# Attention with two feed-forward layers on one core: part of the weight split moved to GpSimd, four raw buffers, held-back stores and a re-planned order

## The chip, the cores and the metric

The kernel runs on one core of one Trainium2 chip. The metric is the device time of one execution in microseconds (us). Engines are named as in the profile: PE is TensorE, DVE is VectorE, ACT is ScalarE, POOL is GpSimd, SP is SyncE, which here only issues DMAs.

## The reference

```python
def reference(**kwargs):
    attn_out = _attn_ref(q, k, v)                 # q, k, v: (4, 8, 576, 64)
    x = attn_out.transpose(0, 2, 1, 3).reshape(B * S, H * D)     # (2304, 512)
    x = _moe_ref(x, moe_w_in, moe_w_out)          # relu(x @ w_in) ** 2 @ w_out
    return _moe2_ref(x, moe2_w_in, moe2_w_out)    # softplus(x @ w_in) @ w_out

# _attn_ref: softmax attention on q, k, v averaged over groups of 4 tokens (144 of them),
# its result repeated 4 times, plus softmax attention over the band |i - j| < 4.
# w_in: (512, 2048), w_out: (2048, 512), all float32.
```

All of it is float32. On PE each product of float32 numbers is made from a high part and a low part in a reduced format (`F32R`): high times high, high times low and low times high, so every weight and every activation is first split in two.

## The kernel before, in words

**Tiles and steps.** The 2304 tokens are 36 groups of 64, cut into five blocks of 8, 6, 6, 8 and 8 groups (`BLOCKS`). A step is one block, one layer and one slice `f` of 128 of the 2048 hidden units: `hidden` multiplies the tokens by that slice of `w_in` (12 matmuls, line 1501), `activate` and `split` make the two parts of the result on ACT and DVE, and `outputs` multiplies by the slice of `w_out` (12 matmuls, line 1585). 106 such steps come first, then two phases that need fewer products (line 1443). Steps 0 to 9 are the first layer on block 0 with the slices 0 to 7, steps 10 to 25 the first layer on block 1.

**Attention.** For blocks 0 and 1 the banded part runs as matmuls (`local`), and so does the pooled part of every batch (`pooled` and `pooled_twos`; their scores are at lines 808 and 894); for blocks 2 to 4 the banded part is done on DVE (`direct`). Block 1 needs the pooled part of batch 1, whose keys, queries and values are added up over 4 tokens by DMAs that accumulate (`token_sums_of`, issued on POOL, line 758).

**Weights.** A slice of a layer's weights is 2 halves (`w_in` and `w_out`), and there are 64 halves. The input holds them as 64-bit numbers. `load_weights` fetches a half of 512 KB into one of `RAWS` buffers (SP, line 500), `weight_job` then does three operations on the raw words, each on ACT or DVE (lines 517 to 533; either engine for the first `ANY_JOBS` halves, ACT alone after that), two on DVE (537 and 540), a copy that makes the high part (either engine) and a subtraction that makes the low part:

```python
copy(w[:, 0], f.tile)
t = yield "dve", t_dve(512)
rest(w[:, 1], f.tile, w[:, 0])
```

The finished half is written to DRAM (SP, line 554), because SBUF has 8 slots for weights, and `weight_again` fetches it from there when it is wanted again (POOL, line 570). `f` has 3 buffers, freed by the subtraction.

**Order.** Nothing is scheduled at run time: each engine's queue is in order, and `Order.run` writes the queues beforehand from a model. Every piece of work is a generator that yields the engine it wants, the time that it is reckoned to take, and what it needs; of what could start first, the planner takes the earliest, then the most urgent. The constants at the top (`LOCAL`, `POOLED`, `U_...`, `NUDGE`, `BIAS`, `AT_ONCE`, `PREP_DVE`, the times behind `yield "pe"`) set urgencies and reckoned times and so the order, not what is computed. `AHEAD` says how many steps ahead of its use a half may be begun. `keep_busy` (line 1206) puts a matmul of the identity, which nobody reads, into PE's queue wherever the model sees PE idle, until step 12; each shows as two instructions. What is in the queue is executed even if PE is late by then.

## Time and profile before

| what | value |
|---|---|
| median of 3 runs | 864.97 us (863.11 to 865.01) |
| the profiled execution | 864.84 us |
| its span, from first to last instruction | 862.9 us |
| matmuls | 4724 |

The profiled execution is 1.9 us longer than its span, and within 0.2 us of the median. In the rows below, times are from the start of the span. A busy PE is not PE at its peak: matmuls are pipelined and their ends are modelled, so the start of one matmul to the start of the next says how long it holds PE.

### The profile page before, as it was taken

Reading aid. Unit: us, or ns where it says so; the run is one execution under the profiler, and the core shown is the slowest. Engines: PE = TensorE matmul, PEld = TensorE weight load, DVE = VectorE, ACT = ScalarE, POOL = GpSimd, SP = SyncE. Lnnn points to the kernel's source line nnn. Section 1 sums busy time; section 2 is a strip of 40 time slices with the busy share of each in tenths; the row PEclk is TensorE's granted clock in tenths of the full one; section 3 lists DMA queues with packets and bytes.
Section 4 is the critical chain, followed back from the end, with each engine's and each line's share of the span. In section 5 each row is a group of like instructions: output and inputs, shape, how many; then the busy total and the mean of one; then the engine's idle time right before and its main releaser. Section 6 shows DMA issues by size and latency. Waiting matters only on the chain.

```text
span 862.9 us, 12987 instructions
## 1 busy us (share of the span) xinstructions
PE 854.3 (99%) x4724; PEld 735.0 (85%) x4724; DVE 691.4 (80%) x1272; ACT 505.3 (59%) x1058; POOL 90.6 (10%) x163
## 2 busy tenths in 40 slices
PE   8999999999999999999999999999999999999998
PEld 5788799988888888899999998888888888888886
DVE  6988989989999899999979999954657497675543
ACT  4967878766997797542336444534454076676500
POOL 0100000010002000122221212012000201100010
PEclk9999999999999999999999999999999999999999
DMA  9996699897769863699995986335210835510161
GB/s 283 243 342 212 228 333 340 299 260 283 262 229 290 288 233 151 192 344 307 295 304 178 309 283 208 118 123 170 74 50 4 283 104 196 157 39 0 52 193 49
DMA packets 49575, 179.20 MB, mean 208 GB/s; under 512 B 5790, under 2 KB 6302, under 8 KB 49512
## 3 DMA queue, kind: packets, MB, share of 16 engines
q1 hardware_dynamic: 27336, 97.92, 32.3%
q0 software_dynamic: 22032, 80.32, 30.9%
q8 instruction: 37, 0.61, 0.3%
q14 instruction: 26, 0.21, 0.1%
q10 hardware_dynamic: 144, 0.13, 0.0%
HBM read 140.08 MB, written 38.27 MB: 207 GB/s over the span
## 4 chain that ended last, share of the span: by engine, by line
PE 98%; DVE 1%; DMA 1%; ACT 0%; issue 0%; SPq 0%; DVEq 0%
PE y L1585 45%; PE ph L1501 28%; PE p L1443 15%; PE idle L1206 1%; PE lsc L996 1%; PE ppo L955 1%; PE lav L1052 1%; PE y L1616 1%; PE ppp L938 1%; PE lpp L1042 1%; PE psc L808 1%; PE dpp L1174 1%; PE psc L894 0%; DMA w_first<-pqk 0%; PE ppo L860 0%; PE ppp L840 0%
## 5 line engine op out<-in xcount | busy, mean ns | idle before, releaser
L1501 PE MATMUL ph<-xh,w 128*128 128x384 f32 (+2 forms) x848 | 248.0, 355 | 0.0
L1585 PE MATMUL y<-gh,w 128*128 128x512 f32 (+2 forms) x640 | 191.0, 365 | 0.2 <-DVE lt L1060 0.2
L1585 PE MATMUL y<-w,gh 128*128 128x512 f32 x576 | 179.4, 392 | 0.0
L1501 PEld LDWEIGHTS ph<-xh,w 128*128 128x128 f32 x848 | 155.7, 188 | 13.7 <-issue 0.2
L1501 PE MATMUL ph<-xl,w 128*128 128x384 f32 (+2 forms) x424 | 149.5, 353 | 0.0
L1585 PEld LDWEIGHTS y<-gh,w 128*128 128x128 f32 x640 | 118.0, 188 | 14.6 <-DVE lt L1060 0.3
L1585 PEld LDWEIGHTS y<-w,gh 128*128 128x128 f32 x576 | 106.8, 188 | 21.9 <-issue 1.0
L570 POOL DMA_DIRECT2D w<-wdram x138 | 73.8, 536 | 483.1 <-PE y L1585 251.1
L1585 PE MATMUL y<-gl,w 128*128 128x512 f32 (+2 forms) x320 | 115.9, 362 | 0.0
L1585 PE MATMUL y<-w,gl 128*128 128x512 f32 x288 | 112.6, 391 | 0.0
L449 DVE TENSOR_TENSOR gl<-g,gh 128x512 fp32r<-128x512 f32 (+2 forms) x162 | 101.9, 629 | 5.2 <-ACT gh L436 2.2
L1501 PEld LDWEIGHTS ph<-xl,w 128*128 128x128 f32 x424 | 79.7, 188 | 6.8
L438 DVE CAST gh<-g 128x512 fp32r<-128x512 f32 (+2 forms) x81 | 32.8, 405 | 50.3 <-PE y L1585 44.4
L1517 ACT ACTIVATE g<-ph 128x384 f32<-128x384 f32 (+2 forms) x58 | 30.3, 522 | 69.8 <-PE ph L1501 69.6
L1585 PEld LDWEIGHTS y<-gl,w 128*128 128x128 f32 x320 | 60.2, 188 | 6.6
L436 ACT ACTIVATE sum<-p 128x512 f32<-128x512 f32 x42 | 24.8, 590 | 69.0 <-PE p L1443 68.9
L436 ACT ACTIVATE gh<-g 128x384 fp32r<-128x384 f32 (+2 forms) x81 | 46.1, 569 | 30.6 <-PE y L1585 18.2
L1585 PEld LDWEIGHTS y<-w,gl 128*128 128x128 f32 x288 | 54.0, 188 | 11.5
L1527 ACT ACTIVATE g<-ph 128x384 f32<-128x384 f32 (+1 forms) x48 | 25.1, 523 | 44.2 <-PE ph L1501 43.9
L1470 DVE TENSOR_TENSOR sum<-p,sum 128x512 f32<-128x512 f32 x42 | 28.9, 687 | 25.4 <-ACT sum L436 17.4
L1160 DVE TENSOR_TENSOR prod<-dv,dsc 128x896 f32<-128x896 f32 x44 | 47.9, 1089 | 0.6
L1167 DVE TENSOR_REDUCE do<-prod 128x128 f32<-128x896 f32 x44 | 47.7, 1084 | 0.8
(183 smaller groups left out, 1428.9 us busy)
## 6 DMA issues: line engine op xcount, KB each, us to landing
w<-wdram POOLq DMA_DIRECT2D x138, 512.0 KB, 4.7
raw<-wts SPq DMA_DIRECT2D x64, 512.0 KB, 5.8
wdram<-w SPq DMA_DIRECT2D x64, 512.0 KB, 5.3
dqk<-dqk SPq DMA_DIRECT2D x11, 896.0 KB, 6.0
dv<-dv SPq DMA_DIRECT2D x11, 640.0 KB, 6.5
qks<-pqs POOLq DMA_DIRECT2D x9, 576.0 KB, 9.3
out<-o SPq DMA_DIRECT2D x17, 256.0 KB, 2.3
vs<-pvs POOLq DMA_DIRECT2D x9, 288.0 KB, 9.4
```

What stands on the lines that cost most here:

```text
L436: act.activation(out=out, in_=in_, func=AF.Copy)
L438: dve.tensor_copy(out=out, in_=in_)
L449: dve.tensor_tensor(out=out, in0=whole, in1=high.bitcast(F32), op=ALU.subtract)
L570: nc.gpsimd.dma_start(out=weights[slot][:, half], in_=wdram[c, half])
L1160: dve.tensor_tensor(out=p4, in0=windows(v4[:, h], 2, t0, p4.shape[1]), in1=s4[:, t0:t0 + some, h].unsqueeze(2).to_broadcast(list(p4.shape) ...
L1167: dve.tensor_reduce(out=o4[:, t0:t0 + some, h], in_=p4, axis=AX.X, op=ALU.add)
L1443: pe.matmul(bank.tile, w, y, start=(k == 0 and p in (1, 2, 5)), stop=(k == len(prs) - 1), skip_group_check=True)
L1470: dve.tensor_tensor(out=b.tile, in0=bank.tile, in1=b.tile, op=ALU.add)
L1501: pe.matmul(ph.tile[:, :n], w, y, start=(k == 0), stop=(k == len(prs) - 1))
L1517: act.activation(out=o, in_=h, func=AF.Relu)
L1527: act.activation(out=o, in_=h, func=AF.Abs)
L1585: pe.matmul(o, wt, y, start=(begin and k == 0), stop=(end and k == 2))
```

## The change

The order constants are set anew (many `NUDGE` entries, `LOCAL`, `BIAS`, `AT_ONCE`, `U_MLP`, `AHEAD`, and the reckoned times of several groups of matmuls). Beside the order, this is changed:

- `RAWS` goes from 3 to 4.
- The stores of halves that belong to steps 0 to 3 (two slices, four halves) are issued once step 4 has begun by the plan; `slot_free` now also tells the planner that a slot can be filled again only when its old content is stored.
- The three raw operations can go to either engine for 40 halves, not 28, and DVE is reckoned at 0.35 for each, not 0.6.
- The first layer's activation can go to either engine for steps below 32 (`BOTH_TO`), not none.
- For the last 36 of the 64 halves (`REST_FROM` is 28) the subtraction that makes the low part is done by POOL.
- The sums of batch 1 begin with the fourth raw load, not the third; those of batches 2 and 3 wait for step 30, not 24. A pair of banded tasks shares its loads whichever of the two comes first.

```diff
--- before.py
+++ after.py
@@ -118,29 +118,32 @@
 
 
 POOLED = [(-20, -17), (-0.6, -0.4), (31, 42), (46, 56)]
-LOCAL = [(-17, -13), (0.5, 6), (14, 46), (46, 64), (58, 74)]
+LOCAL = [(-17, -13), (-2, 4), (14, 46), (46, 64), (58, 74)]
 BY_TWOS = [1, 2, 3]
 
-U_MLP, U_WEIGHTS, U_ATT, U_DIRECT = -2, 0.5, 1, 20
-AHEAD = 10
+U_MLP, U_WEIGHTS, U_ATT, U_DIRECT = -3, 0.5, 1, 20
+AHEAD = 14
 EARLY = 2
 SLOTS = 8
 LENT = 5
 
-RAWS, FLOATS = 3, 3
+RAWS, FLOATS = 4, 3
+STORE_FROM = 4
+REST_FROM, POOL_REST = 28, 1.3
+SUMS_FROM = 3
 LAG = 1
-ANY_JOBS = 28
-PREP_DVE = 0.6
+ANY_JOBS = 40
+PREP_DVE = 0.35
 OUTS = 3
 BUFS = dict(q=2, v=3, s=3, e=4, t=5, pt=2, n=6, do=5)
 BUFS["in"] = 2
 
 LAT = 0.15
-BIAS = 0.1
-NUDGE = {(12, 0): -1, 7: -5, 2: -2, 11: -5, 3: -5, (3, 1): 4, ('l', 2, None): 40, (7, 0): -4, 14: 5, (11, 1): -2, 9: -2, 20: 5, ('at', 2, 2): -0.5}
+BIAS = 0.25
+NUDGE = {7: -5, 3: -5, (3, 1): 4, ('l', 2, None): -2, (7, 0): -4, 14: 5, (11, 1): -2, 9: 5, 20: 5,
...
+    ('l', 7, None): -900, 5: -5, ('l', 8, None): -900, 21: 5, (13, 0): 2, 8: 5, ('at', 11): 0.5, ('at', 8): -2, (10, 0): 4, ('at', 2, 0): 0.5}
 MASKED = 8
-AT_ONCE = 0.5
-BOTH_TO = 0
+AT_ONCE = 2
+BOTH_TO = 32
 PAUSE = 0.2
 WIN, HOT, COLD = 3.413, 3.1, 1.8
 PATIENCE = 0.02
@@ -151,9 +154,9 @@
 FAST_RATE = 4.1e5
 OUTSTANDING = 8
 W_FROM = 1.0
-SUMS_AT = 24
+SUMS_AT = 30
 FIRST_SUMS = [(0, 2, 4, 6), (1, 3, 5, 7, 8)]
-SUM_PE = 0.93
+SUM_PE = 0.94
 
 
 def plan_weights():
@@ -477,6 +480,7 @@
     jobs.sort(key=needed)
     first_fill = [all(y[1] != x[1] for y in fills[:i]) for i, x in enumerate(fills)]
     again = [any(y[1] == x[1] for y in fills[i + 1:]) for i, x in enumerate(fills)]
+    kept_on = {x[1]: any(y[1] == x[1] for y in fills[i + 1:]) for i, x in enumerate(fills) if first_fill[i]}
     stored = {(c, half): Event() for c in range(2 * NF) for half in range(2)}
     landed = {j: Event() for j in jobs}
     w_ready = {j: Event() for j in jobs}
@@ -499,7 +503,7 @@
             b = landed[j].buf = r_raw.take("raw")
             sp.dma_start(out=b.tile, in_=wts[fills[j[0]][1], :, cols(j[1])].bitcast(U32))
             landed[j].at = order.landed(t, 512 << 10)
-            if j == jobs[RAWS - 1]:
+            if j == jobs[SUMS_FROM]:
                 begun.at = t
                 begin_sums(1, t)
 
@@ -544,19 +548,26 @@
             add_slot(wpool, slot)
         w = weights[slot][:, half]
         copy(w[:, 0], f.tile)
-        t = yield "dve", t_dve(512)
-        rest(w[:, 1], f.tile, w[:, 0])
+        if j in jobs[:REST_FROM]:
+            t = yield "dve", t_dve(512)
+            rest(w[:, 1], f.tile, w[:, 0])
+        else:
+            t = yield "pool", POOL_REST
+            nc.gpsimd.tensor_tensor(out=w[:, 1], in0=f.tile, in1=w[:, 0].bitcast(F32), op=ALU.subtract)
         w_ready[j].at = t + 0.1
         f.free = t
         prepared(t)
         if first_fill[j[0]] and again[j[0]]:
-            t = yield "sp", 0.06
+            t = yield "sp", 0.06, step_start(STORE_FROM if fills[j[0]][0] < STORE_FROM else -1)
             sp.dma_start(out=wdram[c, half].bitcast(F32), in_=w.bitcast(F32))
             stored[c, half].at = order.landed(t, 512 << 10)
 
     def slot_free(j):
         (_, _, slot, old), half = fills[j[0]], j[1]
         needs = [lent[slot]] if slot in lent else []
+        before = next((c for _, c, x, _ in fills[:j[0]][::-1] if x == slot), None)
+        if before is not None and kept_on[before]:
+            needs.append(stored[before, half])
         if old[half] is not None:
             needs.append((hidden_done, out_done)[half][old[half]])
         return needs
@@ -615,7 +626,7 @@
         dve.tensor_copy(out=placed[:, 16:32], in_=fours)
         main = rests = None
         for gs in FIRST_SUMS:
-            t = yield "pe", SUM_PE * len(gs) ** 0 * (1 + 0.3 * (len(gs) > 1)), *(first_lv[g // 2] for g in gs), *([] if main else [Two(every)])
+            t = yield "pe", SUM_PE, *(first_lv[g // 2] for g in gs), *([] if main else [Two(every)])
             if not main:
                 main, rests = bank(every, "pvm"), bank(every, "pvr")
             for g in gs:
@@ -697,6 +708,7 @@
             x.buf.left = 2 + min(2, NBLK - 2 * u)
             sp.dma_start(out=x.buf.tile[:KW], in_=lv[u])
             x.at = order.landed(t, KW * 4096, FEWER)
+        loaded = {}
         for (kind, at, hp, i, _), ev in zip(tasks, arrived, strict=True):
             if kind == "d":
                 continue
@@ -707,8 +719,8 @@
                 ev.at = 0.0
                 ev.v.at = first_lv[at // 2].at
             elif kind == "l":
-                if at % 2 == 0:
-                    two = at // 2
+                two = at // 2
+                if two not in loaded:
                     early = two < len(first_lv)
                     t = yield "sp", 0.06, *room(r_q, "q", two), *room(r_k, "k", two), *([] if early else room(r_v, "v", two))
                     bq, bk = (take_for(r, x, two) for r, x in ((r_q, "q"), (r_k, "k")))
@@ -726,7 +738,9 @@
                         t = yield "sp", 0.06
                         sp.dma_start(out=bv.tile[:KW], in_=lv[at // 2])
                         vthere = order.landed(t, KW * 4096, FEWER)
-                ev.buf = bq, bk, bv, at % 2
+                    loaded[two] = bq, bk, bv, there, vthere
+                *bufs, there, vthere = loaded[two]
+                ev.buf = *bufs, at % 2
                 ev.at = there
                 ev.v.at = vthere
             else:
@@ -800,7 +814,7 @@
             dve.tensor_reduce(out=qk.rearrange("p (a g) -> p a g", a=2), in_=x4, axis=AX.X, op=ALU.add)
             used_once(t, ev.buf)
 
-        t = yield "pe", 0.85 if b else 0.5, banks
+        t = yield "pe", 0.85, banks
         sc = bank(banks, "psc")
         sc3 = sc.tile[:, :3 * SP].rearrange("p (i k) -> p i k", i=3)
         for i in range(3):
@@ -831,7 +845,7 @@
         n.free = t
         keys = [(a * KH, KH) for a in range(2)] if b else [(0, 128), (128, SP - 128)]
         for a, (k0, kn) in enumerate(keys):
-            t = yield ("pe", 0.33, banks, r_pt) if a == 0 else ("pe", 0.33, banks)
+            t = yield ("pe", 0.38, banks, r_pt) if a == 0 else ("pe", 0.38, banks)
             if a == 0:
                 pt = r_pt.take("ppt")
                 pt3 = pt.tile.rearrange("p (a k) -> p a k", a=2)
@@ -852,7 +866,7 @@
             yield None, 0.0, first_vd
             sums = first_vd.part
             vds = [sums.tile[:kn, x + hp * 128:x + hp * 128 + 128] for x, (_, kn) in zip((512, 1024), keys)]
-        t = yield "pe", 0.72, banks
+        t = yield "pe", 0.79, banks
         po = bank(banks, "ppo")
         for a, (_, kn) in enumerate(keys):
             pt4 = pt3[:kn, a, :].rearrange("p (i h q) -> p h i q", i=3, h=2)
@@ -885,7 +899,7 @@
         yield None, 0.0, sums_of[b].qk, pace
         qks, vds = zip(*[summed(b, hp + w) for w in range(2)])
         heads = [(w, p) for w in range(2) for p in range(2)]
-        t = yield "pe", 1.2, Two(banks), Two([r_e]), r_n
+        t = yield "pe", 1.26, Two(banks), Two([r_e]), r_n
         es, n = [r_e.take("pe") for _ in range(2)], r_n.take("pn")
         scs = [bank(banks, "psc") for _ in range(2)]
         sc3s = [x.tile[:, :m * SP].rearrange("p (i k) -> p i k", i=m) for x, m in zip(scs, (3, 2))]
@@ -926,7 +940,7 @@
         pts = []
         for a in range(2):
             keys = slice(a * KH, a * KH + KH)
-            t = yield ("pe", 0.57, Two(banks), Two([r_pt])) if a == 0 else ("pe", 0.38, banks)
+            t = yield ("pe", 0.67, Two(banks), Two([r_pt])) if a == 0 else ("pe", 0.46, banks)
             if a == 0:
                 pts = [r_pt.take("ppt") for _ in range(2)]
                 pt4s = [x.tile[:KH].rearrange("p (h q) -> p h q", h=4) for x in pts]
@@ -947,7 +961,7 @@
             t = yield either, t_either(512)
             copy(pt4s[a][:, :, :128], pp.tile[:KH].rearrange("p (h q) -> p h q", h=4))
             pp.free = t
-        t = yield "pe", 1.27, sums_of[b].v, banks
+        t = yield "pe", 1.37, sums_of[b].v, banks
         po = bank(banks, "ppo")
         for h, (w, p) in enumerate(heads):
             for a in range(2):
@@ -1044,7 +1058,7 @@
         t = yield either, t_either(512)
         copy(pt.tile[:KW, :512], pp.tile[:KW, :])
         pp.free = t
-        t = yield "pe", 0.68, ev.v, banks
+        t = yield "pe", 0.6, ev.v, banks
         av = bank(banks, "lav")
         for h in range(NP):
             for a in range(2):
@@ -1168,7 +1182,7 @@
             pr.free = t
         g0 = 2 * u
         bs = sorted({g0 // NBLK, (g0 + 1) // NBLK})
-        t = yield "pe", 0.36, r_a, *(up_ready[b] for b in bs)
+        t = yield "pe", 0.46, r_a, *(up_ready[b] for b in bs)
         pp = r_a.take("dpp")
         for tok in range(FCT):
             pe.transpose(pp.tile[:, tok * 128:(tok + 1) * 128], o.tile[:, tok * 128:(tok + 1) * 128], ident)
```

## Rows read from the trace of the kernel before

**Rows 1.** The page: busy us, share of the span and instructions of each engine.

```profile
PE 854.3 (99%) x4724; PEld 735.0 (85%) x4724; DVE 691.4 (80%) x1272; ACT 505.3 (59%) x1058; POOL 90.6 (10%) x163
```

**Rows 2.** Chain that ended last, in order of time: start us, us, what.

```profile
52.22 2.75 PE ph L1501 x12
...
110.49 2.10 PE ph L1501 x12
...
654.66 35.36 PE y L1585 x156
```

**Rows 3.** Busy time by stretch, all engines: A:B, length, busy (instructions), PE clock, DMA share, GB/s.

```profile
37.80:110.00 72.20, 71.94 (x638) 59.84 (x638) 64.15 (x166) 56.40 (x160) 2.56 (x3) 1.00 0.79 264
110.00:858.00 748.00, 748.00 (x3687) 650.23 (x3686) 597.15 (x1018) 422.89 (x800) 84.18 (x150) 1.00 0.61 200
150.00:350.00 200.00, 200.00 (x1050) 170.26 (x1049) 187.32 (x335) 158.85 (x322) 10.97 (x13) 1.00 0.77 252
```

**Rows 4.** Stretches of the idle matmuls of line 1206 alone: PE and PEld busy (instructions).

```profile
0.00:6.40 6.40, 2.93 (x12) 2.63 (x12) 1.00 0.68 231
6.40:37.80 31.40, 5.25 (x26) 4.13 (x26) 1.00 0.93 265
37.80:110.00 72.20, 6.88 (x42) 5.79 (x42) 1.00 0.79 264
60.00:80.00 20.00, 4.01 (x26) 3.51 (x26) 1.00 0.62 227
110.00:863.00 753.00, 0.99 (x6) 0.96 (x6) 1.00 0.61 200
```

**Rows 5.** Timeline of PE, 37.5 to 38.5 us: the first matmul of `hidden`.

```profile
37.84 0.39 PE L1501 MATMUL ph<-xh,w 128*128 128x256 f32 x1
```

**Rows 6.** Timeline of DVE, 44 to 46 us.

```profile
44.33 0.69 DVE L449 TENSOR_TENSOR w<-f,w 128x512 fp32r<-128x512 f32 x1
```

**Rows 7.** Timeline of PE, 44 to 46 us.

```profile
44.81 0.61 PE L1206 MATMUL idle<-ident 128*128 128x128 f32 x4
45.17 0.36 PE L1501 MATMUL ph<-xh,w 128*128 128x256 f32 x1
```

**Rows 8.** Timeline of ACT, 61 to 74 us.

```profile
71.23 0.38 ACT L914 ACTIVATE pe<-psc,pn 128x144 f32<-128x144 f32 x1 [4.28 <-DVE pn L909]
```

**Rows 9.** Timeline of PE, 61 to 74 us.

```profile
68.75 0.76 PE L894 MATMUL psc<-qks 64*128 64x144 f32 x8
```

**Rows 10.** Groups by line and form, ACT: raw operations, count, busy, mean ns.

```profile
L530 ACT ACTIVATE r<-raw 128x512 int16<-128x512 f32 x60 | 46.8, 782 | 0.0
...
L517 ACT ACTIVATE f<-raw 128x512 f32<-128x512 f32 x54 | 35.7, 665 | 3.0 <-DVE w L449 2.9
```

**Rows 11.** Groups by line and form, DVE: raw operations and the low part of weights.

```profile
L449 DVE TENSOR_TENSOR w<-f,w 128x512 fp32r<-128x512 f32 x64 | 43.7, 687 | 0.5
...
L519 DVE TENSOR_SCALAR f<-raw 128x512 f32<-128x512 f32 x10 | 4.2, 419 | 0.3 <-DMA raw<-wts 0.3
...
L533 DVE TENSOR_SCALAR r<-raw 128x512 uint16<-128x512 uint16 x4 | 1.8, 447 | 0.0
```

**Rows 12.** Groups by line, POOL: the two elementwise instructions that read SBUF.

```profile
L692 POOL CAST mask<-mask 128x210 bf16<-128x210 f32 x1 | 0.4, 362 | 7.5 <-DMA mask<-cmask 7.5
L683 POOL CAST ident<-ident 128x128 bf16<-128x128 f32 x1 | 0.3, 289 | 1.8 <-DMA ident<-cident 1.8
```

**Rows 13.** Timeline of POOL, 0 to 350 us: an accumulating DMA and what it waited for.

```profile
179.67 0.89 POOL L758 DMA_DIRECT2D qks<-pqs  x1 [7.17 <-DMA qks<-pqs]
```

**Rows 14.** Timeline of DVE, 247 to 252 us: the 47th low part.

```profile
248.15 0.68 DVE L449 TENSOR_TENSOR w<-f,w 128x512 fp32r<-128x512 f32 x1
```

**Rows 15.** Timeline of PE, 250.5 to 252 us: the first matmul that reads it.

```profile
251.22 0.34 PE L1501 MATMUL ph<-xh,w 128*128 128x384 f32 x1
```

**Rows 16.** Timeline of SP, 28 to 60 us: the first stores of finished halves.

```profile
30.23 0.33 SPq L554 DMA_DIRECT2D wdram<-w  x1
...
47.87 4.26 SPq L554 DMA_DIRECT2D wdram<-w  x3
```

More of the change, by code (lines that the diff above doesn't have):

```diff
@@ L138 @@
 LAT = 0.15
-BIAS = 0.1
-NUDGE = {(12, 0): -1, 7: -5, 2: -2, 11: -5, 3: -5, (3, 1): 4, ('l', 2, None): 40, (7, 0): -4, 14: 5, (11, 1): -2, 9: -2, 20: 5, ('at', 2, 2): -0.5}
+BIAS = 0.25
+NUDGE = {7: -5, 3: -5, (3, 1): 4, ('l', 2, None): -2, (7, 0): -4, 14: 5, (11, 1): -2, 9: 5, 20: 5, ('at', 2, 2): -1, (12, 1): -4, (0, 0): -1, 2: 2, ('l', 5, None): 1, ('l', 12, None): -2, (15, 0): -1, ('l', 9, None): 1, (13, 1): -4, (7, 1): -1, (1, 1): 1, 16: 5, ('p', 0, 3): 2, ('p', 2, 2): -2, ('p', 0, 0): -2, (8, 1): 1, (3, 0): -1, 18: -5, 1: -5, 17: 2, (15, 1): -4, (6, 0): -8, ('p', 3, 2): 5, ('p', 1, 2): 2, ('l', 11, None): -4, ('l', 3, None): -2, (5, 1): 4, ('l', 10, None): 4, ('l', 13, None): -4, ('at', 9): -0.5, ('at', 1, 2): -1, (2, 0): -2, 0: 5, (12, 0): -2, ('l', 7, None): -900, 5: -5, ('l', 8, None): -900, 21: 5, (13, 0): 2, 8: 5, ('at', 11): 0.5, ('at', 8): -2, (10, 0): 4, ('at', 2, 0): 0.5}
 MASKED = 8
-AT_ONCE = 0.5
-BOTH_TO = 0
+AT_ONCE = 2
+BOTH_TO = 32
 PAUSE = 0.2
```

## The prediction

> **What bounds the kernel now.** I read the busy shares first, then the chain of waits in order of time, then busy time by stretch, and last the timelines of the stretches where PE has nothing to do. [...] From 110 to 858 us PE is busy for 748.00 of 748 us [rows 3]; whatever DVE and ACT do there, PE does not wait for them. So nothing is to be won after 110 us, unless work of PE itself goes away.
>
> What can go away are the matmuls of the identity that the planner puts where its model has PE idle, 86 instructions [rows 4]. Taken from the start of each to the start of PE's next instruction they hold PE for 14.6 us: 3.8 us ahead of 6.4 us, while the first inputs land, 4.7 us up to 37.8 us, where the feed-forward layers begin [rows 5], 5.5 us from there to 110 us, and 0.6 us later. (The busy times of rows 4 are close to these; neighbours overlap there.) What they stand in for is seen twice. At 44.81 us four of them run while DVE makes the low part of a half of weights until 45.02 us, and the step that reads it starts at 45.17 us [rows 6, 7]: PE waits for weights. At 68.75 us PE does the second pair of pooled scores [rows 9]; ACT, whose queue has the exponentials of those scores next, stands idle for 4.28 us until 71.23 us [rows 8], with raw operations behind them in its queue. From 60 to 80 us PE has 26 idle instructions, 4.01 us [rows 4]. The order was written for a PE that is earlier than the real one. From 37.8 to 110 us DVE is busy for 64.15 of 72.2 us and ACT for 56.40 [rows 3], 89% and 78%: neither is full, the chain through both is what PE waits for.
>
> **The change, part by part.**
>
> Shared raw operations. On ACT the first and the last of the three take 665 and 782 ns [rows 10], on DVE 419 and 447 ns [rows 11]: 0.25 to 0.33 us less engine time for each that moves. The first 16 halves, which the first ten steps need, have 48 raw operations, and by the timelines 13 of them are on DVE. With DVE reckoned at 0.35 I expect about half of the other 35 to move: 17 times 0.29 is 5 us of engine time, 2.5 us over two engines that work beside each other. The least is nothing, because DVE is the fuller of the two; the most is 35 times 0.33 over two, 5.8 us. I take 2.5 us: what makes DVE fuller lets the planner give copies, which either may do, to ACT.
>
> The activation on either engine for the first 32 steps and the new order constants. The reckoned times of several of PE's groups rise, so the model has PE later, puts in fewer idle matmuls, and puts an exponential later in ACT's queue, with raw operations ahead of it. The wait of 4.28 us [rows 8] is the nearest row. I take half of the 4.01 us of idle matmuls between 60 and 80 us [rows 4], 2.0 us. The bounds are a loss of 2 us (the new order waits elsewhere, as much again) and a gain of 4 us.
>
> Held-back stores and a fourth raw buffer. Four stores, at 30.23 us and up to the first of the three that begin at 47.87 us in SP's queue [rows 16], move behind the start of step 4, 52.22 us [rows 2]. Raw loads behind them move up, and 4 times 512 KB leave a stretch with 264 GB/s [rows 3], 7.9 us of transfers. But all that DVE waits for raw loads in the whole trace is 0.3 us [rows 11], and PE never waits for one. I take 0.3 us; the most is 2 us, as much as the transfers of one half. What is late next are the stores, and who waits for them are refills of the same slots: not before step 10, 110.49 us [rows 2], so this costs nothing. With that cover gone it would be one landing behind ACT's or DVE's copy.
>
> The other sums after step 30, not 24. They start six steps later, at 24 matmuls of 226.7 ns at the most [rows 2] some 33 us. The block whose pooled part they make is first multiplied in step 63; these 33 steps cover it. Nothing.
>
> GpSimd makes 36 low parts. DVE loses 36 times 687 ns, 24.7 us [rows 11], all of it behind the first 28 halves and so after 110 us, where PE does not wait for DVE: it is worth nothing. What it costs: the trace has no GpSimd instruction with two inputs from SBUF. Its casts take 289 ns for 128 and 362 ns for 210 elements [rows 12], 0.89 ns an element; 512 elements with one input are then 0.63 us (the lower bound), with twice the input 1.26 us (the upper). I take 1.1 us, nearer to the upper because two operands are read. A half is later by 0.4 us, and the distance from a low part to its first use covers it: of the 36 it is least at the 47th half, 2.4 us, from 248.83 to 251.22 us [rows 14, 15]. GpSimd's queue holds the accumulating DMAs too; one waited 7.17 us for the DMA before it [rows 13]. A subtraction behind such a wait makes its half late by up to 7 us, which at the tightest half is up to 5 us of PE; the subtraction also frees `f`, which the next raw operations in ACT's queue want. I take nothing, with these 5 us as the bound, since halves may now begin 14 steps ahead and not 10, and since a model that puts the DMA in its time puts the subtraction before it.
>
> [...]
>
> Sum: 864.84 - 2.5 - 2.0 - 0.3 = 860.0 us for an execution like the profiled one, whose time is within 0.2 us of the median of the runs (864.97 us). These 4.8 us are not quite half of the 10.8 us of idle matmuls after 6.4 us.
>
> **The rivals.**
>
> *Nearly all of the early waiting goes.* If model and chip agree about PE, the 5.5 us after 37.8 us go and half or more of the 4.7 us before it: 8 to 10 us, 855 to 857 us. For it: neither engine is full from 37.8 to 110 us. Against it: the softmax chains of blocks 0 and 1 stay as long as they are.
>
> *The early waiting only moves.* 863 to 866 us. The idle matmuls are as many as before, at other places, or real waits stand where they stood. For it: DVE is at 89% there, and the raw operations go to the fuller engine; the one part with a big saving, 24.7 us of DVE, falls where PE is full anyway.
>
> *GpSimd stops DVE: slower.* From 150 to 350 us, where the last 36 halves are made, DVE is busy for 187.32 of 200 us [rows 3]: 12.7 us are free, and 24.7 us become free. If each of the 36 subtractions holds DVE up for its own length, DVE has time enough up to (12.7 + 24.7) / 36 = 1.04 us each; that is the point that decides. At the upper bound, 1.26 us, DVE lacks 8 us, for which PE waits: 868 us with the early gain, 873 us without. [...]
>
> **How the numbers follow.** Half of the waiting goes, 0.46; nearly all, 0.16; it only moves, 0.20; GpSimd stops DVE or its own queue, 0.18. The predicted time is the first, 860.0 us, with a range of its own of 856 to 862.4. Within 0.3% (2.6 us), about what a measurement of this kernel can tell from no change, is 862.4 to 867.6. So faster is the first two, 0.62; same the third, 0.20; slower the last, 0.18. The range for 8 in 10 leaves out the far end of the second case and most of the last: 854 to 868 us.
>
> **What would show it.** Right: fewer than 60 idle instructions of line 1206; step 4 and step 10 earlier than 52.22 and 110.49 us, the latter by some 5 us; ACT's wait of 4.28 us gone; more than 40 raw operations on DVE; 36 low parts on POOL of 0.63 to 1.26 us; PE busy for all of the stretch from 110 us to its last matmul. Wrong: instructions of DVE with two inputs much longer than 687 ns, or gaps before them, beside those of POOL; waits of PE between 150 and 350 us; as many idle instructions as now; ACT idle at line 517 for an `f` that POOL has not freed.

## The result, and the profile after

The changed kernel takes 874.03 us, median of 4 runs (872.54 to 875.90), beside 864.92 us (863.11 to 865.01) for the kernel before on the same chip: ratio 1.0111, 95% interval [1.0088, 1.0135]. It is slower by 9.1 us, where 860.0 us had been forecast. What came about is the last of the rivals, a little beyond its upper figure. The profiled execution took 875.90 us, the longest of the four and 1.9 us above their median, so what its trace loses is a little more than what the median loses.

From the page of the changed kernel, busy time by engine and the granted clock; beside [rows 1], DVE is less busy by 14.8 us, POOL busier by 53.6, and PE, with fewer matmuls, as busy as before in a span 11.2 us longer. The one 8 in the row of clocks is the slice from 218.5 us on.

```profile
PE 855.2 (98%) x4696; PEld 731.8 (84%) x4696; DVE 676.6 (77%) x1194; ACT 528.3 (60%) x1111; POOL 144.2 (17%) x199
...
PEclk9999999999899999999999999999999999999999
```

**Up to 110 us the change does what was forecast.** The idle matmuls alone (line 1220 here), by the stretches of [rows 4]: 58 instructions where there were 86, and none from 60 to 80 us. From 37.8 to 110 us more data is moved too (296 GB/s for 264).

```profile
6.40:37.80 31.40, 2.64 (x16) 2.09 (x16) 1.00 0.96 275
37.80:110.00 72.20, 4.70 (x28) 3.92 (x28) 1.00 0.88 296
60.00:80.00 20.00, 0.00 (x0) 0.00 (x0) 1.00 1.02 396
110.00:874.00 764.00, 0.38 (x2) 0.38 (x2) 0.99 0.60 193
```

Step 10 begins at 106.67 us, by the timeline of PE; before, its first matmul starts at 110.3 us. Step 4 is not earlier: 53.06 us, beside 52.1. The gain at step 10 is 3.7 us.

```profile
53.06 0.48 PE L1515 MATMUL ph<-xh,w 128*128 128x512 f32 x1
...
106.67 0.33 PE L1515 MATMUL ph<-xh,w 128*128 128x384 f32 x1
```

**Then 14.9 us are lost between 146 and 390 us.** The first phase matmul, which ends the 106 steps, starts at 572.7 us before and at 583.95 us after: the lead of 3.7 us has become a lag of 11.2. Busy time by stretch, in the columns of [rows 3], shows where: PE lacks 2.9 us from 146 to 216 us, 3.6 from there to 229 and 2.0 from there to 390, and in the third row its clock is 0.74. POOL makes the low parts from 146.3 to 328.7 us; PE's last wait, 25 us behind them, is at 353 us. From 110 to 146 us and after 390 PE lacks nothing.

```profile
110.00:146.00 36.00, 36.00 (x209) 36.00 (x209) 34.28 (x69) 29.65 (x55) 0.00 (x0) 1.00 0.91 326
146.00:216.00 70.00, 67.11 (x327) 57.80 (x326) 64.32 (x104) 42.73 (x79) 24.21 (x16) 1.00 0.69 247
216.00:229.00 13.00, 9.40 (x34) 7.55 (x33) 11.49 (x15) 9.34 (x16) 4.63 (x4) 0.74 1.04 350
229.00:390.00 161.00, 158.99 (x840) 132.80 (x839) 149.53 (x238) 117.37 (x251) 41.99 (x41) 1.00 0.74 227
390.00:869.00 479.00, 479.00 (x2262) 414.04 (x2261) 321.77 (x517) 245.34 (x440) 66.93 (x126) 1.00 0.50 160
```

PE's waits after 110 us, 8.5 us in all, are nearly all for DVE (engine and line that waited, whose result; total us, times, longest):

```profile
PE dpp L1188 <- DVE do L1181: 5.1, 2, 3.6
PE y L1599 <- DVE gl L452: 1.7, 4, 0.6
PE y L1599 <- ACT gh L439: 1.2, 3, 0.4
PE ph L1515 <- DVE g L1547: 0.4, 2, 0.2
PE psc L908 <- ACT pe L928: 0.2, 1, 0.2
```

The longest wait costs more than its length. From the timeline of PE:

```profile
222.21 0.69 PE L1188 MATMUL dpp<-ident,do 128*128 128x128 f32 x2 [3.60 <-DVE do L1181]
...
223.55 1.05 PE L1599 MATMUL y<-gh,w 128*128 128x512 f32 x2
```

PE stood for 3.60 us, and the granted clock is then 0.50 from 222.2 to 227.4 us. The matmuls of 512 columns that start from 223.12 to 227.39 us, eleven of them, follow each other at 427 ns and not at 227, which is 2.2 us more.

**Why DVE is late is seen beside POOL's subtractions.** From the timelines of POOL and of DVE:

```profile
191.76 3.17 POOL L556 TENSOR_TENSOR w<-f,w 128x512 fp32r<-128x512 f32 x1 [5.96 <-DVE w L441]
195.29 1.30 POOL L556 TENSOR_TENSOR w<-f,w 128x512 fp32r<-128x512 f32 x1 [0.36 <-DVE w L441]
199.30 2.69 POOL L556 TENSOR_TENSOR w<-f,w 128x512 fp32r<-128x512 f32 x2 [2.71 <-ACT w L439]
```

```profile
199.74 1.07 DVE L1155 TENSOR_TENSOR dsc<-dsc,dn 128x56 f32<-128x56 f32 x1
200.73 1.58 DVE L537 TENSOR_SCALAR r<-raw 128x512 uint16<-128x512 uint16 x1
```

The first of these DVE instructions has a median of 0.22 us and the second 0.46. Each meets one of the two subtractions that run from 199.30 to 201.99 us. By line, with shortest, median and longest duration in ns, the instructions that meet a subtraction are up to about 1.1 us longer than their median, the reductions of line 1181 by nothing, and a subtraction itself takes between 1289 and 3168 ns:

```profile
L541 DVE TENSOR_SCALAR f<-f x64: 376/418/1527, 24.7 to 323.9; 128x512 uint32<-128x512 uint32 x64
```

```profile
L544 DVE CUSTOM_DVE_ANT_0 f<-f,r x64: 659/683/1783, 26.5 to 325.9; 128x1024 uint16<-128x1024 uint16 x64
```

```profile
L1181 DVE TENSOR_REDUCE do<-prod x44: 1068/1082/1087, 161.8 to 546.8; 128x128 f32<-128x896 f32 x44
```

Taken over all DVE instructions that overlap a subtraction, and counting what each has above the median of its form where that is over 0.1 us (called the stretch below), 28 of them are stretched by 21.4 us. So 21.4 of the 24.7 us of subtractions that left DVE came back as longer instructions.

**Each waits for what is left of the other.** One meeting, from the timelines of POOL and of DVE:

```profile
268.43 2.26 POOL L556 TENSOR_TENSOR w<-f,w 128x512 fp32r<-128x512 f32 x1 [3.71 <-PE y L1599]
```

```profile
268.46 1.08 DVE L1174 TENSOR_TENSOR prod<-dv,dsc 128x896 f32<-128x896 f32 x1
269.46 1.78 DVE L544 CUSTOM_DVE_ANT_0 f<-f,r 128x1024 uint16<-128x1024 uint16 x1
```

DVE's product takes its usual time and ends at 269.54 us; the subtraction ends 1.15 us after it, which is why it takes 2.26 us and not 1.29. DVE's next instruction starts while the subtraction runs and ends 0.55 us after it, at 271.24. The other meetings are alike. The ten held instructions of line 544, and of line 452 on 512 columns, end 0.54 to 0.56 us after the subtraction, although they start anywhere from 0.12 to 1.03 us into it, and the nine held shifts and copies of lines 541 and 441 end 0.28 to 0.29 us after it. Of the 21 subtractions that take over 1.33 us, 20 end 1.13 to 1.17 us after a DVE instruction with two inputs, a shift or a copy. Eight of the 36 hold up no DVE instruction, and the others only for what they have left; that makes the mean so much less than a subtraction's length.

PE's longest wait, that for `do` until 222.21 us, follows such a meeting. The product `gl` is held for 1.08 us more than its median, and the reduction behind it in DVE's queue makes the `do`:

```profile
219.27 1.34 POOL L556 TENSOR_TENSOR w<-f,w 128x512 fp32r<-128x512 f32 x1 [1.35 <-ACT w L439]
```

```profile
219.39 1.76 DVE L452 TENSOR_TENSOR gl<-g,gh 128x512 fp32r<-128x512 f32 x1
221.08 1.07 DVE L1181 TENSOR_REDUCE do<-prod 128x128 f32<-128x896 f32 x1
```

### The profile page after: what moved, and what is told of

Same layout as the page of the kernel before. It is cut to its first block, busy times and chain, and to the rows that moved or that the text cites. A ratio compares the mean times of both kernels' runs of the same rounds, so it can differ in the third digit from the quotient of the medians.

```text
span 874.1 us, 13008 instructions
## 1 busy us (share of the span) xinstructions
PE 855.2 (98%) x4696; PEld 731.8 (84%) x4696; DVE 676.6 (77%) x1194; ACT 528.3 (60%) x1111; POOL 144.2 (17%) x199
## 4 chain that ended last, share of the span: by engine, by line
PE 59%; DVE 3%; ACT 0%; issue 0%; DMA 0%; DVEq 0%; ACTq 0%
PE y L1599 30%; PE p L1457 15%; PE ph L1515 12%; DVE prod L1136 1%; PE y L1630 1%; DVE dsc L1143 1%; DVE do L1181 0%; DVE prod L1174 0%; PE dpp L1188 0%; DVE gl L452 0%; PE ppo L969 0%; DMA out<-o 0%; DVE g L1547 0%; ACT pe L928 0%; PE ppp L952 0%
## 5 line engine op out<-in xcount | busy, mean ns | idle before, releaser
L1599 PE MATMUL y<-gh,w 128*128 128x512 f32 (+2 forms) x640 | 193.1, 368 | 1.2 <-ACT gh L439 1.2
L452 DVE TENSOR_TENSOR gl<-g,gh 128x512 fp32r<-128x512 f32 (+2 forms) x162 | 106.5, 657 | 71.0 <-ACT gh L439 68.5
L439 ACT ACTIVATE gh<-g 128x512 fp32r<-128x512 f32 (+2 forms) x143 | 83.6, 584 | 109.7 <-PE y L1599 78.9
L556 POOL TENSOR_TENSOR w<-f,w 128x512 fp32r<-128x512 f32 x36 | 54.5, 1518 | 220.6 <-ACT r L529 100.1
L1531 ACT ACTIVATE g<-ph 128x384 f32<-128x384 f32 (+2 forms) x54 | 28.3, 523 | 50.9 <-PE ph L1515 46.2
L544 DVE CUSTOM_DVE_ANT_0 f<-f,r 128x1024 uint16<-128x1024 uint16 x64 | 48.2, 756 | 4.6 <-ACT r L534 3.3
L1136 DVE TENSOR_TENSOR prod<-dqk 128x896 f32<-128x896 f32 x44 | 48.6, 1103 | 0.4
```

Of the source, the lines that this page charges most:

```text
L439: act.activation(out=out, in_=in_, func=AF.Copy)
L452: dve.tensor_tensor(out=out, in0=whole, in1=high.bitcast(F32), op=ALU.subtract)
L544: dve.tensor_tensor(out=f.tile.bitcast(I32), in0=f.tile.bitcast(I32), in1=r.tile, op=ALU.add)
L556: nc.gpsimd.tensor_tensor(out=w[:, 1], in0=f.tile, in1=w[:, 0].bitcast(F32), op=ALU.subtract)
L1136: dve.tensor_tensor(out=p4, in0=windows(k4[:, h], 1, t0, p4.shape[1]), in1=q4[:, h, t0:t0 + some].unsqueeze(2).to_broadcast(list(p4.shape) ...
L1531: act.activation(out=o, in_=h, func=AF.Relu)
```

## The experiments

The theory: GpSimd's reads hold up DVE's instructions, and DVE's lateness is what PE waits for. Its rivals: the subtraction's own time on POOL makes halves, and `f`, late; or the new order would be slow with no GpSimd work at all. The "before" median beside which each ratio was taken lies between 864.5 and 864.9 us.

### Who does the low parts: e1, e2

e1 takes the change but for the move to GpSimd; e2 takes the kernel before and that move alone. Both are planned anew by the kernel's own planner.

```diff
 # e1, on the changed kernel
-REST_FROM, POOL_REST = 28, 1.3
+REST_FROM, POOL_REST = 64, 1.3
 # e2, on the kernel before
-        t = yield "dve", t_dve(512)
-        rest(w[:, 1], f.tile, w[:, 0])
+        if j in jobs[:28]:
+            t = yield "dve", t_dve(512)
+            rest(w[:, 1], f.tile, w[:, 0])
+        else:
+            t = yield "pool", 1.3
+            nc.gpsimd.tensor_tensor(out=w[:, 1], in0=f.tile, in1=w[:, 0].bitcast(F32), op=ALU.subtract)
```

> The changed kernel with all 64 low parts on DVE again (REST_FROM 64); the planner writes a new order for it. Theory A (beside a GpSimd subtraction DVE instructions are stretched, 21 us in the trace after, and this is what PE pays for): PE waits between 110 and 400 us go, the 3.7 us won by step 10 stay, about 861 us. Theory B (the new order and constants are what is too tight, whoever makes the low parts): DVE gets 24.7 us of work more, PE still waits as in the changed kernel, 872 us or more. Theory C (only the later half through GpSimd's own queue and the three f buffers matter): also about 861 us.

> The kernel before with one edit: the last 36 low parts by GpSimd, planned at 1.3 us each; order constants of before. Theory A: DVE instructions beside the subtractions are stretched by some 20 us in all and PE waits after 150 us for 8 to 15 us: 872 to 880 us. Theory B: the order of before has room, PE does not wait, 863 to 867 us.

e1: 863.19 us, ratio 0.9986 [0.9977, 0.9996]; step 10 at 105.8 us, PE waits for 2.0 us after 110. e2: 882.66 us, 1.0215 [1.0188, 1.0241]; DVE is stretched by 23.6 us in 27 instructions. e1 is 2 us above what theory A expected of it, and e2 beyond the 872 to 880 us. Either way round, the version with GpSimd is slower, by 10.8 and by 18.0 us. But an order is planned anew in both, and the runs on the early gain below show what that alone can cost; so the next runs keep the changed kernel's own order, instruction for instruction, and vary only what POOL does in its 36 places.

### The same order, other work on GpSimd: e3, e4, e5

e3 keeps about the time on POOL and takes the reads of SBUF away but for 32 columns; e4 takes half of the time away too; e5 gives the subtraction to DVE, where the planner does not know of it.

```diff
-            nc.gpsimd.tensor_tensor(out=w[:, 1], in0=f.tile, in1=w[:, 0].bitcast(F32), op=ALU.subtract)
 # e3: the same on columns 0 to 16, two memsets, the same on columns 496 to 512
+            nc.gpsimd.tensor_tensor(out=w[:, 1, :16], ...)
+            nc.gpsimd.memset(w[:, 1, 16:496].bitcast(F32), 0.0)
+            nc.gpsimd.memset(w[:, 1, 16:496].bitcast(F32), 0.0)
+            nc.gpsimd.tensor_tensor(out=w[:, 1, 496:], ...)
 # e4
+            nc.gpsimd.memset(w[:, 1, :496].bitcast(F32), 0.0)
+            nc.gpsimd.tensor_tensor(out=w[:, 1, 496:], ...)
 # e5
+            rest(w[:, 1], f.tile, w[:, 0])
```

> The changed kernel in its own order, every engine's queue the same but for GpSimd: each of the 36 subtractions is replaced by a subtraction of the first 16 columns, two memsets of the 480 columns between, and a subtraction of the last 16, so GpSimd is busy for about as long (1.0 to 1.5 us) and frees f as late, but reads almost nothing. The low parts of those 36 halves are left out but for 32 columns (zeros). Theory A: no stretched two-input DVE instructions, PE waits mostly gone, 860 to 863 us. Theory B: 872 to 875 us as in the changed kernel, since the order is the same. Theory C: between, some 868 us, since f is freed as late.

> As the run before it, but with one memset of 496 columns and a subtraction of the last 16, so that GpSimd is done in about half the time. The low parts of those 36 halves are left out but for 16 columns. Theory A: the same as the run before it, 860 to 863 us; the length of GpSimd's work does not matter while it does not read. Theory B: 872 to 875 us. Theory C: clearly faster than the run before it, 860 against 868 us.

> The changed kernel in its own order, with the 36 subtractions given to DVE at the same places of the order, where the plan has no time for them: 24.7 us more for DVE, no GpSimd instruction beside it. If PE only pays for the time that DVE loses (21.4 us stretched in the changed kernel, 24.7 us here), 872 to 876 us. If PE pays for how that time is lost (single instructions of DVE and the f buffers 1 to 3 us late) and not for its sum, 860 to 866 us.

e3: 864.49 us, 0.9995 [0.9985, 1.0004]. e4: 860.50 us, 0.9954 [0.9937, 0.9971]. e5: 870.21 us, 1.0059 [1.0044, 1.0074]. So 9.5 us of the change's time go when GpSimd reads 32 of 512 columns and does its work in four shorter pieces, although POOL then has more to do. Two expectations were missed: e3 is 1.5 us above the 860 to 863 us of theory A, and e4, for which theory A expected the same time as e3, is 4.0 us faster. e5 fell between its two. Groups by line of e3, POOL: 67.4 us of elementwise work, where line 556 of the changed kernel has 54.5.

```profile
L558 POOL MEMSET w<- 128x480 f32 x36 | 19.1, 530 | 2.1
L557 POOL MEMSET w<- 128x480 f32 x36 | 18.2, 506 | 0.0
L559 POOL TENSOR_TENSOR w<-f,w 128x16 fp32r<-128x16 f32 x36 | 15.4, 429 | 0.0
L556 POOL TENSOR_TENSOR w<-f,w 128x16 fp32r<-128x16 f32 x36 | 14.7, 409 | 198.6 <-ACT r L529 101.7 <-ACT w L439 73.3 <-DVE w L441 23.1
```

By line in e3, the instruction with two inputs is no longer held (762 ns at most, where it was 1783); the shift of line 541 still is, a little, beside a memset:

```profile
L544 DVE CUSTOM_DVE_ANT_0 f<-f,r x64: 660/686/762, 26.8 to 314.5; 128x1024 uint16<-128x1024 uint16 x64
```

```profile
L541 DVE TENSOR_SCALAR f<-f x64: 377/419/883, 25.0 to 312.1; 128x512 uint32<-128x512 uint32 x64
```

In e4 PE does not wait once after 110 us; busy time of its stretch from there to 390 us:

```profile
110.00:390.00 280.00, 280.00 (x1486) 246.58 (x1485) 256.46 (x441) 205.22 (x408) 52.42 (x104) 1.00 0.81 266
```

So the order itself is sound, which rules out the second rival. Against e4, whose step 10 starts 0.4 us earlier, the changed kernel has lost 15.5 us at the first phase matmul. As both have the same matmuls in the same order, the starts can be compared one by one. The lag of 0.4 us stays until 146 us, is 5.9 us at 216, grows by 3.8 at the wait of 3.60 us and by 2.7 up to 228.2 us, where the clock is low, and by 3.1 more until 354 us; after that it stays. Of the 15.0 us in between, 12.3 thus arise at PE's waits and 2.7 at the lower clock. The waits alone read 8.5 us because the profile counts idle time from the modelled end of the matmul before, and because it lists no gap below 0.15 us: where it has 0.60 us of idle time at 199.30 us, that matmul and the next start 0.99 us later.

e5 bears on the reserve by which the forecast judged. The 36 subtractions, 24.7 us of DVE [rows 11], cost 9.7 us more than e4 at places where the planner had not counted them, and 2.7 us more where it had (e1, though in an order planned anew).

### Is it `f`, or a read of one input: e6, e9, e15

ACT waits 6.9 us for `f` that POOL has not freed, once 5.8 us (timeline of ACT, changed kernel):

```profile
194.96 0.67 ACT L521 ACTIVATE f<-raw 128x512 f32<-128x512 f32 x1 [5.81 <-POOL w L556]
```

e6 and e9 give the changed kernel and e3 a fourth buffer for `f` that the planner does not know of. e15 is e9 with the memsets replaced by copies that read one input.

```diff
 # e6 on the changed kernel, e9 on e3
-    r_f = ring(prep, "f", [128, 512], FLOATS)
+    r_f = Ring(lambda name: prep.tile([128, 512], F32, tag="f", name=name, bufs=FLOATS + 1), FLOATS)
 # e15 on e9, twice
-            nc.gpsimd.memset(w[:, 1, 16:496].bitcast(F32), 0.0)
+            nc.gpsimd.tensor_copy(out=w[:, 1, 16:496], in_=f.tile[:, 16:496])
```

> The changed kernel in its own order, but f has four buffers behind the three that the planner knows, so that an f which GpSimd frees late holds up ACT and DVE no more. If the late f is what costs PE most of it, 864 to 868 us; if it is the 4 us by which the shorter GpSimd work was faster, 869 to 871 us; if it is the stretched DVE instructions alone, 873 to 875 us.

> The run in which GpSimd is busy as long but reads only 32 columns of each of the 36 halves (their low parts are left out but for those), in the same order, with a fourth f buffer that the planner does not know. It was 4.0 us slower than the run with half of that GpSimd work. If those 4 us are an f freed late, which stops ACT and DVE: 860 to 861.5 us. If they are memsets that hold up DVE's fast copies and shifts (3.5 us stretched there, 2.4 us with the shorter work): 863.5 to 865 us.

> The kernel of e9 (the order of the change, a fourth f buffer) with the wide memset of each GpSimd low part replaced by a GpSimd copy of the same 480 columns of f, so one input instead of two or none; the low parts of the 36 halves are left out but for 32 columns each. If any GpSimd read of SBUF holds VectorE's two-input forms, VectorE's instructions beside them are stretched by 10 to 20 us in all and the time is 868 to 873 us. If only the two-input subtraction does it, the stretch stays under 7 us and the time is 861 to 863 us.

e6: 873.63 us, 1.0103 [1.0088, 1.0118]; ACT no longer waits for POOL's `f`, and PE's longest wait is still 3.6 us; that is the time expected of the stretched instructions alone. e9: 861.62 us, 0.9966 [0.9953, 0.9979], just above the 860 to 861.5 us expected of a late `f`. e15: 867.95 us, 1.0037 [1.0024, 1.0050]. A late `f` is worth 2.9 us where DVE is free (e3 to e9) and nothing where it is held (e6). Between e9, e15 and e6, which have the same order and the same buffers:

| | POOL's time on low parts | DVE's stretch | PE's waits after 110 us | median |
|---|---|---|---|---|
| e9, memsets | 74.8 us | 4.8 us | 0.8 us | 861.62 us |
| e15, one input | 90.4 us | 12.6 us | 3.9 us | 867.95 us |
| e6, two inputs | 55.1 us | 22.5 us | 8.6 us | 873.63 us |

The time follows DVE's stretch and not POOL's own time, which is the least where the kernel is slowest. That rules out the first rival as the main cause. e15 shows that a read of one input holds DVE too, at the lower end of the 10 to 20 us expected of it, and its 867.95 us are just under the 868 to 873. In e9 and e15 POOL works in four pieces each, and neither ACT nor DVE waits there for an `f` that POOL has not freed, so the 6.3 us between them go with the read of one input (and with copies of 0.8 us where the memsets take 0.5); the 5.7 us from e15 to e6 go with the single, longer instruction and its second input, which no run here takes apart. By line, e15, POOL's two copies are 0.8 us each, and DVE's two-input instruction goes to 1122 ns, not 1776 as in e6:

```profile
L558 POOL CAST w<-f 128x480 fp32r<-128x480 f32 x36 | 28.8, 799 | 2.2
L557 POOL CAST w<-f 128x480 fp32r<-128x480 f32 x36 | 27.6, 767 | 0.0
```

```profile
L544 DVE CUSTOM_DVE_ANT_0 f<-f,r x64: 664/689/1122, 26.0 to 318.0; 128x1024 uint16<-128x1024 uint16 x64
```

Its longest hold, 433 ns above the median, is shorter than the copy. Here too a held instruction of line 544 ends 0.54 us after the piece that it meets; the longest hold of that line in e6 is 1093 ns.

### Where PE's longest wait could be avoided: e12

e1 still has one wait of 1.6 us before the transposes of line 1188. e12 plans them 2 us later.

```diff
-        t = yield "pe", 0.46, r_a, *(up_ready[b] for b in bs)
+        there = Event()
+        there.at = t + 2.0
+        t = yield "pe", 0.46, r_a, there, *(up_ready[b] for b in bs)
```

> The run with all low parts on DVE, with the transposes of the direct attention planned 2 us after DVE has made their input (a new order). In that run one wait of PE for it, 1.6 us at 223 us, was the largest after 110 us. If such waits are what it gives back of its early gain: 860 to 862 us, step 10 at 105.8 us as there. If the new order only moves the waits: 863 us or more.

863.34 us, 0.9991 [0.9981, 1.0001]: no gain over e1, as expected if the new order only moves the waits.

### Where the early gain comes from: e7, e8, e10, e11, e13, e14, e16, e17

With all low parts on DVE (e1 and the kernel before), the change has three parts: the loads (fourth raw buffer, held-back stores, first sums at the fourth load), the shared work (raw operations and activation), and the order's constants.

```diff
 # the loads, taken away in e7 (all), e10 (RAWS, SUMS_FROM) and e11 (STORE_FROM); alone in e13
-RAWS, FLOATS = 4, 3
-STORE_FROM = 4
+RAWS, FLOATS = 3, 3
+STORE_FROM = 0
-SUMS_FROM = 3
+SUMS_FROM = 2
 # the shared work, taken away in e8; alone in e14; with the loads in e16; both taken away in e17
-ANY_JOBS = 40
-PREP_DVE = 0.35
+ANY_JOBS = 28
+PREP_DVE = 0.6
-BOTH_TO = 32
+BOTH_TO = 0
```

> The run with all low parts on DVE, with three raw buffers, no store held back and the sums of batch 1 as before (three constants set back, new order). By the prediction's 0.3 us for these parts: within 1.5 us of that run, 862 to 865 us, and step 10 within 1 us of its 105.8 us. If the early gain comes from the loads: step 10 at 108 to 110 us and 865 to 868 us.

> The run with all low parts on DVE, with the raw operations shared as before (28 halves, reckoned at 0.6 on DVE) and the activation on ACT alone (three constants set back, new order). By the prediction's 2.5 us for shared raw operations and part of the 2.0 us: step 10 is 2.5 to 4.5 us later than there, at 108 to 110 us, and the time 865 to 868 us. If the order constants alone made the gain: step 10 within 1 us of 105.8 us.

> The run with all low parts on DVE, with three raw buffers and the sums of batch 1 from the third raw load (a new order). Of the three constants that together made step 10 8 us later, this has two. If the buffer is what matters: idle instructions of PE well above 58, step 10 at 111 us or later, 868 us or more. If it is the stores: step 10 within 1 us of 105.8 us, 862 to 865 us.

> The run with all low parts on DVE, with the stores of the first four halves not held back (a new order). If the stores are what matters: step 10 at 110 us or later, 867 us or more, more than 58 idle instructions. If it is the buffer: step 10 within 1 us of 105.8 us, 862 to 865 us.

> The kernel before with the fourth raw buffer and the stores held back, and nothing else: the raw operations and the order's constants stay those of before. If earlier loads give the early gain by themselves, step 10 begins 2 to 5 us earlier than the 110.3 us of before and the time is 860 to 863 us. If they give it only together with constants fitted to them, step 10 begins within 1.5 us of 110.3 and the time is 864 to 868 us.

> The kernel before with the raw operations shared out to VectorE through the early jobs and the activation on either engine, and nothing else: three raw buffers and the stores as before. The forecast's own terms ask for step 10 some 4 us earlier than 110.3 us and 860 to 862 us. The theory that the loads bind there asks for step 10 within 1.5 us of 110.3 and 863 to 867 us.

> The kernel before with the loads of e13 and the shared raw operations of e14 together, and the order's constants of before. If the parts bring the gain once they are together, step 10 begins 3 to 5 us earlier than 110.3 us and the time is 860 to 863 us. If only the constants fitted to them bring it, step 10 is at 110 us or later and the time is 865 to 875 us, as in e13 and e14.

> The kernel before with the new order constants and the shared loads of a banded pair alone: three raw buffers, stores and sums as before, raw operations and activation shared out as before, all low parts on VectorE. If the constants bring the gain by themselves, step 10 begins before 108 us and the time is 861 to 864 us. If they bring it only with the buffers and stores that they were fitted to, step 10 is at 111 us or later and the time is 867 to 873 us, as in e7.

All eight combinations, the median and the start of step 10 (the kernel before: 110.3 us):

| | constants of before | new constants |
|---|---|---|
| neither | before: 864.97, 110.3 | e17: 870.56, 116.0 |
| shared work | e14: 874.57, 113.5 | e7: 870.68, 113.9 |
| loads | e13: 869.83, 111.8 | e8: 863.61, 107.4 |
| both | e16: 871.41, 113.2 | e1: 863.19, 105.8 |

Ratios: e7 1.0064 [1.0047, 1.0081], e8 0.9986 [0.9977, 0.9996], e13 1.0064 [1.0047, 1.0080], e14 1.0115 [1.0098, 1.0132], e16 1.0070 [1.0053, 1.0086], e17 1.0070 [1.0054, 1.0086]. e10 gave 868.06 us, 1.0041 [1.0027, 1.0055], step 10 at 111.3; e11 gave 867.19 us, 1.0032 [1.0016, 1.0047], step 10 at 110.1.

Beside the runs of the kernel before that go with each, the loads alone lose 5.1 us and the constants alone 5.9; with the constants in place the loads bring step 10 forward by 8.6 us (e17 to e8) and 8.1 (e7 to e1), without them by nothing (1.5 us later in e13, 0.3 earlier from e14 to e16). The shared work gives nothing: e8 is 1.5 us behind e1 at step 10 and level with it from step 13 on (116.8 us in both). With loads and constants together more data is moved from 37.8 to 110 us and PE has fewer idle matmuls: those of line 1220, first of e17, then of e1 (the last two columns are the DMA share and GB/s).

```profile
37.80:110.00 72.20, 9.73 (x56) 7.84 (x57) 1.00 0.84 275
```

```profile
37.80:110.00 72.20, 4.69 (x28) 3.92 (x28) 1.00 0.88 294
```

More data alone does not do it: e13 moves 283 GB/s there, and its step 10 is no earlier. Which wait the loads lift was not traced.

Of the expectations, those came true that the buffer (e10) and the stores (e11) matter, and that the parts need the fitted constants (e16) and the constants the parts (e17). e7 is 2.7 us slower than the slower of its two; e8 lies between its two; e13 missed both, with 869.83 us where 864 to 868 had been the slower; of e14 both were too low, the forecast's by over 12 us. These runs also bound what any single run planned anew can say: of the nine orders here beside that of the kernel before, seven are 2 to 10 us slower, though each has only options added or taken away. The loss of e2 holds such a share too, of unknown size.

## Why the prediction was wrong

**The early part, right in size by luck and wrong in its parts.** Of 4.8 us forecast, 3.7 came at step 10 (4.5 in e1). The idle matmuls fell to 58, ACT's wait of 4.28 us [rows 8] is now 0.97 us, and 55 raw operations run on DVE. But the term of 2.5 us for them is worth about nothing (e8), and the term of 0.3 us for the loads was read from DVE's waits for raw data [rows 11]; e10 and e11 put step 10 5.4 and 4.2 us later for taking either half of it away, in an order fitted to both. That DVE hardly waits in the trace did not show that a fourth buffer is worth nothing; that the order had been arranged around three fits e13, where a fourth brings nothing in that order. The constants, given 2.0 us together with the shared activation, bring step 10 forward by 4.4 and 7.4 us where the loads are in place (e13 to e8, e16 to e1), and by nothing without them. Step 4, forecast to be earlier, was 1.0 us later.

**The step that failed: GpSimd's low parts at nothing.** The forecast said "it is worth nothing" of the relief and "I take nothing" of the cost. The relief is worth some 2.7 us where DVE is hardly held (e4 beside e1, in different orders). The subtraction alone was just above its upper bound (1.29 us at the least, beside 1.26), and the queue of accumulating DMAs, for which 5 us had been kept as a bound, was not the trouble: e9, with more work in that queue, takes 861.62 us; a late `f` is worth 2.9 us at most (e3 to e9), and twice the work on POOL 1.1 us beside that (e4 to e9). What it costs is DVE, held by reads: 9.5 us (e3 to the change) to 12.0 us (e9 to e6), of which 6.3 come with a read of one input in four pieces (e9 to e15).

**The rival had the mechanism and the wrong point of decision.** It let each subtraction hold DVE for 1.04 us before DVE would lack time, by adding up 12.7 us of idle DVE and 24.7 us freed. Measured, the hold is 21.4 / 36 = 0.59 us for each subtraction, well inside that, and yet the kernel is 13.5 us slower than with the short memsets of e4, where the rival had priced the loss at 8. The sum treated DVE's time as a pool. Two things are wrong with that. The freed 24.7 us were no reserve: the new order was written with them, so other work of DVE stands in their place: from 110 to 390 us DVE is busy for 260.7 us before, and in e4, which moves the 36 subtractions off DVE and hardly holds it, still for 256.46, with 8 us more of raw operations and some 12 us more of the direct attention. And a hold of 1.1 us strikes an instruction that a certain matmul waits for, in order behind it, whatever is idle 20 us later: the same 24.7 us cost 9.7 us unplanned (e5) and 2.7 planned (e1). PE's longest wait, behind the `gl` held at 219.39 us, is such a case.

**What is held and what is not** stood in no row of the trace before; the rival's 0.18 was the author's estimate. Held beside the 36 subtractions of the changed kernel were DVE instructions with two inputs from SBUF (lines 452, 544 and 1136, up to 1.09, 1.10 and 0.87 us above their median), shifts (lines 537 and 541, up to 1.13 and 1.11 us) and two copies of line 441 (0.10 and 0.11 us). The fifteen reductions that meet a subtraction stay within 13 ns of their median, and the instruction of line 1547, whose input `ph` is in PSUM, takes its usual 0.68 us at 283.83 us, inside a subtraction that starts at 283.71. In e3, where GpSimd only writes but for 32 columns, two-input instructions go free (762 ns at most on line 544) and the shifts are still held, up to 883 ns; the runs do not show why. In the meetings shown above one waits for the other, in both directions: a held DVE instruction ends 0.55 us (two inputs of 512 columns) or 0.28 us (a shift of line 541) after the subtraction, wherever it began, and a held subtraction ends 1.13 to 1.17 us after the DVE instruction.

**What stays open:** how much of the price is the second input and how much the length of one instruction (e15 to e6); which wait the loads lift; and which of the many constants work with the loads, as they were tried only all together.

## What to carry to other kernels

Before moving elementwise work from VectorE to GpSimd, count which VectorE instructions will run beside it and read two tensors from SBUF, or are shifts and casts, which were the ones held here: 0.59 us came back for each 0.69 us moved, and nothing in the trace before showed it. In a kernel whose queues are written beforehand, time freed on an engine is not a reserve, since the new order has already spent it; judge a hold by the instruction that it strikes and who waits for that. And a resource that nobody waits for in the trace may be one that the order was bent around, so an edit that lifts it has to be tried with the order fitted to it: here the loads alone lost 5 us, the fitted constants alone 6, and both together won 1.3 (e8).

The version that beats both kernels is e1, the change with all low parts on VectorE: 863.19 us, 0.9986 [0.9977, 0.9996] of the time before.

## What the runs showed of the hardware

In the changed kernel a GpSimd subtraction of 128x512 takes 1289 ns at the least, 1360 at the median and 3168 at the worst: it is held as well as holding, and the longest ends 1.16 us after the last of four DVE instructions that follow one behind the other from 191.55 to 193.77 us. A DVE instruction held by it ends 0.54 to 0.56 us after it with two inputs of 512 columns (lines 452 and 544), and 0.28 to 0.29 us after it for the shift of line 541. Small instructions of DVE are held too: the normalisation of 128x56 numbers above took 1.07 us and not 0.22. Two GpSimd copies of one input of 128x480, 0.8 us each, in the place of each subtraction held DVE about half as much in all (e15 beside e6, 12.6 and 22.5 us), though POOL was busy with the low parts for longer (90.4 and 55.1 us). And one wait of 3.60 us was followed by 5.2 us at half the clock, 2.7 us on top of the wait beside the same matmuls in e4.
